# Batch 0 of a mixing-and-maxout kernel: other load order, other split of its reversed copies, more table matmuls, and a second PSUM bank for the last half block

## The chip, the cores and the metric

The kernel runs on one core of one Trainium2 chip. The core has a matrix engine (TensorE, PE in the profile), a vector engine (VectorE, DVE), a scalar engine (ScalarE, ACT), GpSimd (POOL) and SyncE (SP), which here only starts transfers. Transfers are started on three queues: SP's and ACT's (hardware queues, q1 and q10 in the profile) and POOL's (the software queue, q0). The metric is the device time of one execution in microseconds (us); lower is better.

## What is computed

The input `x` has 8 batches of 3072 x 256 numbers. Each batch goes through a two-dimensional Fourier transform of which only the real part is kept. The result, 24576 rows of 256, goes through a feed-forward layer whose hidden values are the maximum of three products.

```python
X = np.fft.fft(x, axis=1)
X = np.fft.fft(X, axis=2)
attn_out = X.real.astype(np.float32)
x = attn_out.reshape(B * S, D)
h = np.maximum(np.maximum(x @ w1, x @ w2), x @ w3)
return (h @ w_out).astype(np.float32)
```

## The kernel before

**Factoring.** The transform over 3072 rows is split as 24 times 128. Stage "s" (`Mix.s`, lines 406 to 427) does the 24-point part together with the four column groups of 64, stage "k" (`Mix.k`, 429 to 447) the 128-point part with a table of sines and cosines (`tab`). The transform over the 256 columns is folded into the weights of the layer: `prep_first` (352) and `prep_second` (373) multiply the weights with a table `md_all` and its negative `nmd_all`. After that each batch is three blocks of six units (`unit_plus`, `unit_minus`, `unit_out`), and each block is followed by its output layer (`l2_block`, 489, and `l2_last`, 532, for the last block of the last batch). A written plan (`plan`, `at`) says after which unit the stages of the next batch, the turning of its input and the loads of the batch after that are issued. Each engine then works through its own list in the order of the program.

**Input of a batch.** In memory on the chip a batch lies as 96 partitions: 4 column groups of 24 rows each. A partition holds 128 rows `bb` of 64 numbers `dl`. Stage "s" uses a column `d` twice: as it is (line 415, from `x`) and as the mirrored column of the rows in reverse order (line 417, from `back`). So a reversed copy is made: row `bb` goes to place 129 - r0 - m onward, and only `dl` 32 to 64 are needed. The reversed order also needs the row after the last one, which is the first row of the next partition: `load_next` (103) fetches these single rows in five transfers, four of 23 partitions and one of 4 partitions.

**Batch 0** is handled by code of its own, at the head of the program.

- Rows 0 to 79 come on POOL's queue, cast to bf16 on the way, straight into `x0_first` (lines 178, 186, 190), four transfers per group of rows, one per column group; then come the weights (195, 200).
- Rows 80 to 127 come as float32 on the hardware queues into three staging tiles `xs` (160 to 170): rows 80 to 95 on SP, 96 to 111 on ACT, then on SP the five one-row transfers of `load_next` and after them rows 112 to 127.
- VectorE makes the angles of `tab` (236), ScalarE the sines (249); then the small tables follow, and the angles `vm` of `md_all` (309 to 326).
- Lines 330 to 339 finish the input. For each staging tile VectorE casts it into `x0_first` (331) and ScalarE makes the reversed copy (332, recorded at line 130 in `reverse`). Then ScalarE makes the sines `md_all` (333), and five more pieces are reversed out of `x0_first`: ScalarE takes (rows 80 on, `dl` 64), (rows 0 to 30) and the lower `dl` of rows 63 to 79; VectorE takes rows 31 to 62 and the upper `dl` of rows 63 to 79.
- Before its first real work TensorE runs 17 matmuls on the table whose result is not used (line 610). The first real pair is the matmul of line 415 for column 2 and the one of line 417 behind it; 33 such pairs make stage "s" of batch 0, in seven groups; the first group needs `dl` 58 to 62 of the reversed copy, the second 53 to 57, and so on down.

**The order around the change.** A hardware transfer is given one of eight completion semaphores in turn, counted over SP and ACT together. A ninth transfer is issued when the first has landed. POOL's transfers have eight of their own.

**The end.** `l2_last` writes the last 512 rows and their mirror rows in four parts (sub 3, 0, 1, 2). Each part has two halves `h` in one PSUM tile `po` of 512 columns: six matmuls each (line 485), after two short ones (548, 550). For the last part (sub 2) each half is copied out on its own (line 554) and stored on its own (564).

Of the kernel before, what the change touches and what calls it, by code (L numbers as in the profile page):

```python
# [9 lines left out]
FP32 = mybir.dt.float32  # L10
BF16 = mybir.dt.bfloat16
# [22 lines left out]
def kernel(  # L34
# [9 lines left out]
    nc = tc.nc  # L44
# [16 lines left out]
    ps_f = ctx.enter_context(tc.tile_pool(name="ps_f", bufs=2, space=bass.MemoryType.PSUM))  # L61
    xs_pool = ctx.enter_context(tc.tile_pool(name="xs", bufs=4))
# [30 lines left out]
    def x_rows(b):  # L93
        return x[b].rearrange("(a bb) (g dl) -> g a bb dl", bb=128, g=4)

    def load_rows(eng, dst, b, r0, r1, after=None):
        xr = x_rows(b)
        for g in range(4):
            ld = eng.dma_start(out=dst[g * 24:(g + 1) * 24], in_=xr[g, :, r0:r1, :])  # L99
            if after is not None:  # L100
                tc.add_manual_dep(ld.ins, after.ins.name, AFTER, reason="weights first")

    def load_next(eng, dst, b, after=None):

        xr = x_rows(b)
        parts = [(dst[g * 24: g * 24 + 23], xr[g, 1:24, 0:1, :]) for g in range(4)]
        parts.append((dst[23:96:24], xr[:, 0, 0:1, :]))
        for (to, src) in parts:
            ld = eng.dma_start(out=to, in_=src)
            if after is not None:  # L110
                tc.add_manual_dep(ld.ins, after.ins.name, AFTER, reason="weights first")

    def load_chunk(b, ch, after=None):
        xs = xs_pool.tile([96, 33 * 64], FP32, name="xs", tag="xs")
        xv = xs.rearrange("p (bb dl) -> p bb dl", dl=64)
        load_rows(nc.sync, xv[:, 0:32 if ch == 3 else 33, :], b, ch * 32,
                  ch * 32 + (32 if ch == 3 else 33), after)
        if ch == 3:
            load_next(nc.sync, xv[:, 32:33, :], b, after)
        return xs  # L120
# [4 lines left out]
    def reverse(copy, xr, xs, r0, n, d0=32, d1=65):  # L125

        last = r0 + n > 128
        for (lo, hi, m) in ((d0, min(d1, 64), n), (64, d1, n - 1)) if last else ((d0, d1, n),):
            if lo < hi:
                copy(out=xr[:, lo - 32:hi - 32, 129 - r0 - m:129 - r0],  # L130
                     in_=bass.AP(xs.tensor, xs.offset + (m - 1) * 64 + lo,
                                 [xs.ap[0], [1, hi - lo], [-64, m]]))
# [19 lines left out]
    gen = gen_pool_cm.__enter__()  # L152
# [6 lines left out]

    x0_first = x0_pool.tile([96, 64 * 130], BF16, name="x0", tag="x0")  # L160
    x0v = x0_first.rearrange("p (bb dl) -> p bb dl", dl=64)
    staged = []
    for (r0, eng) in ((80, nc.sync), (96, nc.scalar), (112, nc.sync)):
        n = 17 if r0 == 112 else 16
        xs = xs_pool.tile([96, 33 * 64], FP32, name="xs", tag="xs")
        xv = xs[:, 0:n * 64].rearrange("p (bb dl) -> p bb dl", dl=64)
        if n > 16:
            load_next(eng, xv[:, 16:17, :], 0)
        load_rows(eng, xv[:, 0:16, :], 0, r0, r0 + 16)
        staged.append((r0, n, xs))  # L170

    pidx = gen.tile([128, 1], FP32, tag="pidx")
    iota(pidx, [[0, 1]], cm=1)
# [19 lines left out]
    for jh in range(2):  # L193
        for wsrc, wdst in ((moe_w1, w1_bf), (moe_w2, w2_bf), (moe_w3, w3_bf)):
            wld = nc.gpsimd.dma_start(
                out=wdst.rearrange("p (fc j) -> p fc j", fc=2)[:, :, jh * 384:(jh + 1) * 384],
                in_=wsrc.rearrange("(fc p) j -> p fc j", fc=2)[:, :, jh * 384:(jh + 1) * 384])
        if jh == 0:
            first_half = wld
    nc.gpsimd.dma_start(out=wout_bf.rearrange("p (jc c) -> p jc c", jc=NJC),  # L200
                        in_=moe_w_out.rearrange("(jc p) c -> p jc c", jc=NJC))
# [19 lines left out]
    half = gen.tile([128, 256], FP32, tag="half")  # L221
# [35 lines left out]
    def tab_minus(r0, r1):  # L257
        nc.vector.tensor_scalar(out=tabs[:, r0:r1, 2, :], in0=tabs[:, r0:r1, 0, :],
                                scalar1=-1.0, scalar2=None, op0=ALU.mult)
# [36 lines left out]
    for (m, c, by) in ((m24f, 0, ind24), (m24r, 24, ind24[:, ::-1])):  # L296
        nc.vector.tensor_tensor(
            out=m.rearrange("p (g r) -> p g r", g=4),
# [7 lines left out]

    tab_minus(0, 7)

    vm = gen.tile([128, 512], FP32, tag="vm")
    qm = gen.tile([128, 512], FP32, tag="qm")  # L310
    pf = gen.tile([128, 2], FP32, tag="pf")
    half = gen.tile([128, 256], FP32, tag="half")
    nc.vector.memset(half[:, 0:128], 64.0)
    nc.vector.memset(half[:, 128:256], 0.0)
    for fc in range(2):
        nc.vector.tensor_scalar(out=pf[:, fc:fc + 1], in0=pidx, scalar1=float(128 * fc),
                                scalar2=None, op0=ALU.add)
# [1 line left out]
            out=vm[:, fc * 256:(fc + 1) * 256].rearrange("p (k c) -> p k c", c=128),  # L319
# [5 lines left out]
    nc.vector.scalar_tensor_tensor(out=vm, in0=qm, scalar=-256.0 * ROUND, in1=vm,  # L325
                                   op0=ALU.add, op1=ALU.subtract)

    back = gen.tile([96, 33 * 130], BF16, tag="back")
    xr0 = back.rearrange("p (dl bb) -> p dl bb", bb=130)
    for (r0, n, xs) in staged:  # L330
        nc.vector.tensor_copy(out=x0_first[:, r0 * 64:(r0 + n) * 64], in_=xs[:, 0:n * 64])
        reverse(nc.scalar.copy, xr0, xs, r0, n, 32, 64)
    nc.scalar.activation(out=md_all, in_=vm, func=AX.Sin, scale=float(-2.0 * math.pi / 256.0))
    for (copy, r0, n, d0, d1) in ((nc.scalar.copy, 80, 49, 64, 65),
                                  (nc.scalar.copy, 0, 31, 32, 65),
                                  (nc.vector.tensor_copy, 31, 32, 32, 65),
                                  (nc.scalar.copy, 63, 17, 32, 49),
                                  (nc.vector.tensor_copy, 63, 17, 49, 65)):
        reverse(copy, xr0, x0_first[:, r0 * 64:(r0 + n) * 64], r0, n, d0, d1)
    nc.vector.tensor_scalar(out=nmd_all, in0=md_all, scalar1=-1.0, scalar2=None, op0=ALU.mult)  # L340
    tab_minus(7, 13)
    nc.vector.tensor_scalar(out=sgn, in0=pidx, scalar1=0.0, scalar2=None, op0=ALU.is_equal)
# [135 lines left out]
    def stored(st, mine, others):  # L478
        for group in others:
            tc.declare_no_dep(st.ins, group=group, reason="each store has rows of its own")  # L480
        tc.add_to_no_dep_group(mine, st.ins)

    def l2_hidden(po, hcols):
        for jc in range(NJC):
            nc.tensor.matmul(po, hcols(jc), wout_bf[:, jc * 256:(jc + 1) * 256],  # L485
                             start=False, stop=(jc == NJC - 1), skip_group_check=True)
            yield
# [44 lines left out]
    def l2_last(hp, hm, te, to, flipped):  # L532

        base = (B - 1) * S
        ter, tor = flipped
        for sub in (3, 0, 1, 2):
            slot = 8 + sub
            r = slot + 1
            cp = slice(slot * 128, slot * 128 + 128)
            sp = slice(sub * 128, sub * 128 + 128)  # L540
            sm = slice((3 - sub) * 128, (4 - sub) * 128)
            po = ps_o.tile([128, 512], FP32, name="po", tag="po")
            ot = out_pool.tile([128, 512], FP32, name="ot", tag="ot")
            for (h, tev, tov, wo, hid) in (
                    (0, te[:, cp], to[:, cp], gw[:, 256:512], lambda jc: hp[:, jc, sp]),
                    (1, ter[:, sm], tor[:, sm], gw[:, 512:768], lambda jc: hm[:, jc, sm])):
                ph = po[:, h * 256:(h + 1) * 256]
                nc.tensor.matmul(ph, tev, gw[:, 0:256], start=True, stop=False)
                yield
                nc.tensor.matmul(ph, tov, wo, start=False, stop=True)  # L550
                yield
                yield from l2_hidden(ph, hid)
                if sub == 2:
                    nc.vector.tensor_copy(out=ot[:, h * 256:(h + 1) * 256], in_=ph)
            if sub != 2:
                nc.vector.tensor_copy(out=ot, in_=po)
            if r <= 11:
                stores = [(0, 128, base + r, 0), (0, 128, base + 24 - r, 256)]
            else:
                stores = [(0, 64, base, 0), (64, 128, base + 12, 0),  # L560
                          (0, 64, base + 1548, 256), (64, 127, base + 1560, 256)]
            for k, (p0, p1, row, c) in enumerate(stores):
                eng = nc.scalar if sub == 2 and k == 0 else nc.sync
                stored(eng.dma_start(out=out[row: row + 24 * (p1 - p0 - 1) + 1: 24, :],
                                     in_=ot[p0:p1, c:c + 256]), "direct", ("scattered",))
# [40 lines left out]
                l2_queue.pop(0)  # L606

    warm = ps_s.tile([128, 512], FP32, name="warm", tag="ps")
    for _ in range(17):
        nc.tensor.matmul(warm, tab[:, 0:128], tab[:, 0:512], start=True, stop=True)  # L610
    m = Mix(0)
    x0f = (lambda d: x0v[:, 0:128, d], rows_back(xr0))
# [150 lines left out]
```

## Time and profile before

| | us |
|---|---|
| runs of the kernel before | 428.53, 429.80, 429.81 |
| median of them | 429.8 |
| the profiled execution | 428.75 |
| its span, first to last instruction | 427.0 |
| TensorE busy in it | 407.5 (95%) |
| VectorE, ScalarE, GpSimd busy | 274.1, 258.1, 244.3 |
| first real matmul of batch 0 | starts at 19.65 |
| its partner, from the reversed copy | starts at 20.65 |

The profile is of one execution. Its views name an instruction by engine, line and tiles: "L130 ACT back<-x" is the reversed copy of line 130, done by ScalarE. A number in brackets behind a row is the idle time of that engine before it and what ended it. Times in a timeline count from the start of the span, and so does every time of day in this text. The execution's own time is 1.75 us longer than the span, for what lies around it.

### The profile page before, as it was taken

Reading aid. Unit: us, or ns where it says so; the run is one execution under the profiler, and the core shown is the slowest. Engines: PE = TensorE matmul, PEld = TensorE weight load, DVE = VectorE, ACT = ScalarE, POOL = GpSimd, SP = SyncE. Lnnn points to the kernel's source line nnn. Section 1 sums busy time; section 2 is a strip of 40 time slices with the busy share of each in tenths; the row PEclk is TensorE's granted clock in tenths of the full one; section 3 lists DMA queues with packets and bytes.
Section 4 is the critical chain, followed back from the end, with each engine's and each line's share of the span. In section 5 each row is a group of like instructions: output and inputs, shape, how many; then the busy total and the mean of one; then the engine's idle time right before and its main releaser. Section 6 shows DMA issues by size and latency. Waiting matters only on the chain.

```text
span 427.0 us, 8732 instructions
## 1 busy us (share of the span) xinstructions
PE 407.5 (95%) x3073; PEld 271.5 (64%) x3073; DVE 274.1 (64%) x455; ACT 258.1 (60%) x477; POOL 244.3 (57%) x291
## 2 busy tenths in 40 slices
PE   0699999999999999999999999999999999999996
PEld 0275667666676666666666666666666666666665
DVE  8747566565666665676656665675656665666773
ACT  6736666666666666656665566647665666655550
POOL 9639655973279625983289624983289622214320
PEclk9989999999999999999999999999999999999999
DMA  9998893594217941498217851387311221212223
GB/s 131 130 170 176 169 230 111 141 217 103 98 72 169 202 134 52 109 206 168 99 61 169 207 141 51 96 199 179 107 55 71 64 74 63 74 51 58 93 74 124
DMA packets 130180, 52.28 MB, mean 122 GB/s; under 512 B 112081, under 2 KB 127192, under 8 KB 130136
## 3 DMA queue, kind: packets, MB, share of 16 engines
q1 hardware_dynamic: 107784, 36.52, 36.6%
q0 software_dynamic: 20624, 14.68, 15.0%
q10 hardware_dynamic: 1728, 0.52, 0.6%
q8 instruction: 24, 0.39, 0.4%
q14 instruction: 20, 0.16, 0.1%
HBM read 29.02 MB, written 25.17 MB: 127 GB/s over the span
## 4 chain that ended last, share of the span: by engine, by line
PE 94%; POOL 2%; DMA 2%; ACT 1%; DVE 0%; issue 0%; POOLq 0%
PE po L485 29%; PE pse L461 15%; PE pse L462 15%; PE pse L469 14%; PE po L509 5%; PE ps L415 3%; PE ps L417 3%; PE ps L443 3%; PE ps L441 2%; PE pl L501 2%; POOL x L99 2%; DMA x<-in_x_dram 2%; PE psg L361 1%; ACT back L130 0%; PE pst L380 0%
## 5 line engine op out<-in xcount | busy, mean ns | idle before, releaser
L475 ACT ACTIVATE stmp<-pse 128x512 bf16<-128x512 f32 x288 | 171.5, 600 | 52.7 <-PE pse L462 47.0
L519 POOL DMA_INDIRECT out_dram<-ot,rows_m x92 | 100.4, 1091 | 160.7 <-DVE ot L514 145.0
L476 DVE TENSOR_TENSOR hp<-pse,stmp 128x512 bf16<-128x512 f32 x144 | 99.5, 691 | 129.8 <-ACT stmp L475 91.4
L461 PE MATMUL pse<-t,gE 128*128 128x512 bf16 x288 | 109.2, 379 | 1.0 <-ACT gO L368 0.6
L462 PE MATMUL pse<-t,gO 128*128 128x512 bf16 x288 | 109.0, 378 | 0.0
L476 DVE TENSOR_TENSOR hm<-pse,stmp 128x512 bf16<-128x512 f32 x144 | 99.2, 689 | 6.8 <-ACT stmp L475 6.7
L485 PE MATMUL po<-wout_bf,hp 128*128 128x256 bf16 x576 | 86.1, 273 | 0.0
L469 PE MATMUL pse<-t,gD 128*128 128x512 bf16 x288 | 85.6, 379 | 0.0
L485 PE MATMUL po<-wout_bf,hm 128*128 128x256 bf16 x576 | 78.6, 273 | 0.0
L485 PEld LDWEIGHTS <-hp 128*128 128x128 bf16 x576 | 56.4, 98 | 26.1
L485 PEld LDWEIGHTS <-hm 128*128 128x128 bf16 x576 | 56.4, 98 | 16.3
L514 DVE TENSOR_TENSOR ot<-po,even 128x512 f32<-128x512 f32 x92 | 62.8, 683 | 0.0
L145 POOL CAST x<-xs 96x1056 bf16<-96x1056 f32 (+1 forms) x35 | 58.3, 1677 | 0.0
L143 POOL CAST x<-xs 96x1056 bf16<-96x1056 f32 x28 | 56.7, 2027 | 0.0
L445 ACT CAST t<-ps 128x512 bf16<-128x512 f32 x47 | 27.5, 586 | 43.3 <-PE ps L443 43.1
L422 ACT CAST z_all<-ps 128x480 bf16<-128x480 f32 x45 | 25.2, 559 | 43.1 <-PE ps L417 43.1
L469 PEld LDWEIGHTS <-gD 128*128 128x128 bf16 x288 | 27.9, 98 | 32.2
L462 PEld LDWEIGHTS <-gO 128*128 128x128 bf16 x288 | 28.1, 98 | 20.4 <-issue 2.0
L461 PEld LDWEIGHTS <-gE 128*128 128x128 bf16 x288 | 28.1, 98 | 19.5 <-issue 0.4
L509 PE MATMUL po<-gw,t 128*128 128x512 bf16 x92 | 34.9, 379 | 0.0
L415 PE MATMUL ps<-m24f,x 96*128 96x96 bf16 (+1 forms) x256 | 29.8, 213 | 2.0 <-DMA w_bf<-in_moe_w_dram 2.0
L415 PEld LDWEIGHTS <-x 96*128 96x128 bf16 x264 | 25.3, 106 | 3.0 <-DVE back L130 2.5
(137 smaller groups left out, 325.4 us busy)
## 6 DMA issues: line engine op xcount, KB each, us to landing
xs<-in_x_dram SPq DMA_DIRECT2D x84, 198.0 KB
out_dram<-ot SPq DMA_DIRECT2D x90, 128.0 KB
xs<-in_x_dram SPq DMA_DIRECT2D x28, 192.0 KB
out_dram<-ot,rows_m POOLq DMA_INDIRECT x92, 2.9
w_bf<-in_moe_w_dram POOLq DMA_DIRECT2D x6, 192.0 KB, 5.7
out_dram<-ot SPq DMA_DIRECT2D x17, 64.0 KB
xs<-in_x_dram SPq DMA_DIRECT2D x8, 96.0 KB
x<-in_x_dram POOLq DMA_DIRECT2D x8, 96.0 KB, 7.9
```

What stands on the lines that cost most here:

```text
L143: nc.gpsimd.tensor_copy(v[:, 0:33, ch * 32:ch * 32 + 32], xs[:, 0:32 * 64].rearrange("p (bb dl) -> p dl bb", dl=64)[:, 0:33, :])
L145: reverse(lambda out, in_: nc.gpsimd.tensor_copy(out, in_), v[:, 33:66, :], xs, ch * 32, 33 if ch == 3 else 32)
L415: nc.tensor.matmul(ps1[:, c0:c0 + n], x0[0](d), mf[:, 0:n], start=True, stop=False)
L461: nc.tensor.matmul(pse[:, 0:n], gE[i][:, js], te, start=True, stop=False)
L462: nc.tensor.matmul(pse[:, 0:n], gO[i][:, js], to, start=False, stop=True)
L469: nc.tensor.matmul(pse, gD[i][:, js], to, start=False, stop=True, skip_group_check=True)
L475: nc.scalar.activation(out=stmp[:, 0:n], in_=pses[0][:, 0:n], func=AX.Relu)
L476: nc.vector.tensor_tensor(out=dst, in0=src3, in1=stmp[:, 0:n], op=ALU.max)
L485: nc.tensor.matmul(po, hcols(jc), wout_bf[:, jc * 256:(jc + 1) * 256], start=False, stop=(jc == NJC - 1), skip_group_check=True)
L509: nc.tensor.matmul(po, to[:, cp], gw[:, 256:768], start=True, stop=True)
L514: nc.vector.tensor_tensor(out=ot.rearrange("p (h c) -> p h c", h=2), in0=po.rearrange("p (h c) -> p h c", h=2), in1=lin.unsqueeze(1).to_br ...
L519: stored(nc.gpsimd.indirect_dma_start(out, bass.IndirectOffsetOnAxis(ap=rows_m[0:128 - lo, b * 12 + slot: b * 12 + slot + 1], axis=0), ot[ ...
```

## The change

Four things are changed at the head and one at the end.

1. Loads of rows 80 to 127. Rows 112 to 127 go to ACT's queue, as its only loads. On SP the four one-row transfers of 23 partitions come first, then rows 80 to 111 as four transfers of 32 rows into one staging tile, then the one-row transfer of 4 partitions. There are two staging tiles now: `xs_a` with 17 rows (112 to 127 and the one-row transfers) and `xs_b` with 32 rows.
2. The casts of the staging tiles into `x0_first` move from VectorE to ScalarE, and their reversed copies from ScalarE to VectorE.
3. VectorE does these reversed copies ahead of the angles `vm`, not behind them. The five later pieces are split in another way: ScalarE takes rows 0 to 30 ahead of the sines `md_all`, and `dl` 54 to 64 of rows 31 to 79 behind them; VectorE takes the rest. A second tile of constants (two memsets) falls away.
4. 27 table matmuls in place of 17.
5. In `l2_last` the second half of the last part gets a PSUM tile of its own, out of another pool.

```diff
--- before.py
+++ after.py
@@ -100,12 +100,14 @@
             if after is not None:
                 tc.add_manual_dep(ld.ins, after.ins.name, AFTER, reason="weights first")
 
-    def load_next(eng, dst, b, after=None):
+    def load_next(eng, dst, b, after=None, mid=None):
 
         xr = x_rows(b)
         parts = [(dst[g * 24: g * 24 + 23], xr[g, 1:24, 0:1, :]) for g in range(4)]
         parts.append((dst[23:96:24], xr[:, 0, 0:1, :]))
-        for (to, src) in parts:
+        for k, (to, src) in enumerate(parts):
+            if k == 4 and mid is not None:
+                mid()
             ld = eng.dma_start(out=to, in_=src)
             if after is not None:
                 tc.add_manual_dep(ld.ins, after.ins.name, AFTER, reason="weights first")
@@ -159,15 +161,12 @@
 
     x0_first = x0_pool.tile([96, 64 * 130], BF16, name="x0", tag="x0")
     x0v = x0_first.rearrange("p (bb dl) -> p bb dl", dl=64)
-    staged = []
-    for (r0, eng) in ((80, nc.sync), (96, nc.scalar), (112, nc.sync)):
-        n = 17 if r0 == 112 else 16
-        xs = xs_pool.tile([96, 33 * 64], FP32, name="xs", tag="xs")
-        xv = xs[:, 0:n * 64].rearrange("p (bb dl) -> p bb dl", dl=64)
-        if n > 16:
-            load_next(eng, xv[:, 16:17, :], 0)
-        load_rows(eng, xv[:, 0:16, :], 0, r0, r0 + 16)
-        staged.append((r0, n, xs))
+    xs_a, xs_b = [xs_pool.tile([96, 33 * 64], FP32, name="xs", tag="xs") for _ in range(2)]
+    rows = lambda t, r0, r1: t[:, r0 * 64:r1 * 64].rearrange("p (bb dl) -> p bb dl", dl=64)
+    load_rows(nc.scalar, rows(xs_a, 0, 16), 0, 112, 128)
+    load_next(nc.sync, rows(xs_a, 16, 17), 0, mid=lambda: load_rows(
+        nc.sync, rows(xs_b, 0, 32), 0, 80, 112))
+    staged = [(112, 17, xs_a), (80, 32, xs_b)]
 
     pidx = gen.tile([128, 1], FP32, tag="pidx")
     iota(pidx, [[0, 1]], cm=1)
@@ -306,12 +305,19 @@
 
     tab_minus(0, 7)
 
+    back = gen.tile([96, 33 * 130], BF16, tag="back")
+    xr0 = back.rearrange("p (dl bb) -> p dl bb", bb=130)
+
+    def turn_rows(copy, r0, n, d0, d1):
+        reverse(copy, xr0, x0_first[:, r0 * 64:(r0 + n) * 64], r0, n, d0, d1)
+
+    for (r0, n, xs) in staged:
+        nc.scalar.copy(out=x0_first[:, r0 * 64:(r0 + n) * 64], in_=xs[:, 0:n * 64])
+        reverse(nc.vector.tensor_copy, xr0, xs, r0, n, 32, 64)
+
     vm = gen.tile([128, 512], FP32, tag="vm")
     qm = gen.tile([128, 512], FP32, tag="qm")
     pf = gen.tile([128, 2], FP32, tag="pf")
-    half = gen.tile([128, 256], FP32, tag="half")
-    nc.vector.memset(half[:, 0:128], 64.0)
-    nc.vector.memset(half[:, 128:256], 0.0)
     for fc in range(2):
         nc.vector.tensor_scalar(out=pf[:, fc:fc + 1], in0=pidx, scalar1=float(128 * fc),
                                 scalar2=None, op0=ALU.add)
@@ -325,18 +331,12 @@
     nc.vector.scalar_tensor_tensor(out=vm, in0=qm, scalar=-256.0 * ROUND, in1=vm,
                                    op0=ALU.add, op1=ALU.subtract)
 
-    back = gen.tile([96, 33 * 130], BF16, tag="back")
-    xr0 = back.rearrange("p (dl bb) -> p dl bb", bb=130)
-    for (r0, n, xs) in staged:
-        nc.vector.tensor_copy(out=x0_first[:, r0 * 64:(r0 + n) * 64], in_=xs[:, 0:n * 64])
-        reverse(nc.scalar.copy, xr0, xs, r0, n, 32, 64)
+    turn_rows(nc.scalar.copy, 0, 31, 32, 65)
+    turn_rows(nc.vector.tensor_copy, 80, 49, 64, 65)
     nc.scalar.activation(out=md_all, in_=vm, func=AX.Sin, scale=float(-2.0 * math.pi / 256.0))
-    for (copy, r0, n, d0, d1) in ((nc.scalar.copy, 80, 49, 64, 65),
-                                  (nc.scalar.copy, 0, 31, 32, 65),
-                                  (nc.vector.tensor_copy, 31, 32, 32, 65),
-                                  (nc.scalar.copy, 63, 17, 32, 49),
-                                  (nc.vector.tensor_copy, 63, 17, 49, 65)):
-        reverse(copy, xr0, x0_first[:, r0 * 64:(r0 + n) * 64], r0, n, d0, d1)
+    for (r0, n) in ((31, 32), (63, 17)):
+        turn_rows(nc.scalar.copy, r0, n, 54, 65)
+        turn_rows(nc.vector.tensor_copy, r0, n, 32, 54)
     nc.vector.tensor_scalar(out=nmd_all, in0=md_all, scalar1=-1.0, scalar2=None, op0=ALU.mult)
     tab_minus(7, 13)
     nc.vector.tensor_scalar(out=sgn, in0=pidx, scalar1=0.0, scalar2=None, op0=ALU.is_equal)
@@ -544,6 +544,8 @@
             for (h, tev, tov, wo, hid) in (
                     (0, te[:, cp], to[:, cp], gw[:, 256:512], lambda jc: hp[:, jc, sp]),
                     (1, ter[:, sm], tor[:, sm], gw[:, 512:768], lambda jc: hm[:, jc, sm])):
+                if sub == 2 and h == 1:
+                    po = ps_f.tile([128, 512], FP32, name="pol", tag="ps")
                 ph = po[:, h * 256:(h + 1) * 256]
                 nc.tensor.matmul(ph, tev, gw[:, 0:256], start=True, stop=False)
                 yield
@@ -606,7 +608,7 @@
                 l2_queue.pop(0)
 
     warm = ps_s.tile([128, 512], FP32, name="warm", tag="ps")
-    for _ in range(17):
+    for _ in range(27):
         nc.tensor.matmul(warm, tab[:, 0:128], tab[:, 0:512], start=True, stop=True)
     m = Mix(0)
     x0f = (lambda d: x0v[:, 0:128, d], rows_back(xr0))
```

## The prediction, made before the changed kernel was run

> **What bounds the kernel now.** I read the page first. TensorE is busy 95% of the span, and the slices of the second part put its idle time at the head:
>
> ```profile
> PE   0699999999999999999999999999999999999996
> PEclk9989999999999999999999999999999999999999
> ```
>
> The first slice has no matmul, the last is short, and the clock dips in the third. TensorE's waits after 29 us sum to 1.3 us, 0.5 of it at the end. So in between nothing absorbs or adds time: what the head gives or takes reaches the end whole, and so does the tail.
>
> Next I read the chain of waits up to 32 us. It follows POOL's loads of x, then a DMA landing, then ScalarE's reversed copies, then the first pair:
>
> ```profile
> 12.04 6.55 DMA x<-in_x_dram
> 18.58 2.02 ACT back L130 x2
> 20.60 0.05 issue
> 20.65 0.22 PE ps L417
> ```
>
> ScalarE's timeline shows what stands ahead of that copy:
>
> ```profile
> 16.88 1.18 ACT L130 CAST back<-xs 96x544 bf16<-96x544 f32 x1 [2.82 <-DMA xs<-in_x_dram]
> 17.96 0.63 ACT L333 ACTIVATE md_all<-vm 128x512 bf16<-128x512 f32 x1
> ```
>
> ScalarE sits idle 2.82 us until the last staging tile has landed at 16.88. From then it works without a gap to 20.59, and TensorE starts at 20.65: **3.77 us from landing to start.** Rows 0 to 30 were in long before; they only stand behind in ScalarE's list.
>
> Why does it land that late? SyncE's list of issues, then packets, MB and share of the queues in the stretches 8:10 (one line) and 11:16 (us):
>
> ```profile
> 0.74 1.81 SPq L99 DMA_DIRECT2D xs<-in_x_dram  x4
> 3.76 3.04 SPq L109 DMA_DIRECT2D xs<-in_x_dram  x5
> ```
>
> ```profile
> q1 hardware_dynamic: 61, 0.02, 4.9%
> ```
>
> ```profile
> q0 software_dynamic: 3293, 0.32, 106.4%
> q1 hardware_dynamic: 1413, 0.35, 47.3%
> ```
>
> After four transfers each on SP and ACT, the ninth waits for the first landing (3.76). Then q1 carries almost only one-row packets in 8:10, while rows 112 on are queued behind them. In 11:16 it moves 283 packets per us beside POOL's queue.
>
> **The loads.** The new order gives the eight completion slots to ACT's four transfers (rows 112 to 127) and four one-row transfers. SP's first 32-row transfer is the ninth and waits for ACT's first. In before the first landed 3.0 us after its issue at 0.74, so I expect about 3.7 again, and its packets from about 5.0 (1.25 us after issue: the first packets of before show just before 2.0). These four transfers are 4 x 24 x 32 = 3072 packets of 256 B. The fifth one-row transfer (1 KB) is behind them in the same queue, and **both the cast and the reversed copy of `xs_a` read its row**. So `xs_a`, first in both engines' lists, can be taken up only when `xs_b` lands too. Call that time L.
>
> Bounds for L. Slow end: 283 packets per us throughout, 10.9 us, plus 0.8 from the last packets to the casts (about 16.05, as 16:17 holds only 14 more, to 16.88): 16.7. [...] Alone, q1 moved 846 in 28:29 (14 ns per packet on each of the 12 engines that a 24-partition load lands on by the trace's DMA events); alone, q0 moved 1409 in 8:9 (11 ns on 16). [...] I take 15.3: POOL's queue has only half the hardware loads ahead of it and so gets a start, which leaves q1 about 390 per us (midway from 283 to the 496 of 5:6) for 3 us, and 283 after that. This is nearer to the slow end, whose row has the same queues on the same engines.
>
> [...]
>
> **From L to the first pair.** ScalarE's list in after: cast 1088 numbers, cast 2048, reversed copy of rows 0 to 30, sines, two pieces of 352 and 187. Casts by L253's rows (896 in 0.95, 768 in 0.84, so 0.9 ns per number): 1.12 and 1.99. Rows 0 to 30 cost 1.94 and the sines 0.63, as now. The pieces lie between rows of 48 (0.26), 289 (0.68) and 512 (1.08): 0.79 and 0.50. That is 6.97, less five overlaps of about 0.09: 6.5, plus 0.06 to TensorE. **The start is L + 6.6**, against 3.77 behind the landing now: more of ScalarE's work stands behind it. For L = 15.3 it is 21.9, later by 1.25 us.
>
> VectorE's copies of the staging tiles have no row. The nearest are bf16 copies of its own (1056 in 1.13, 272 in 0.40), so 0.65 and 1.10; ScalarE's 512 float32 in 1.06 gives 1.13 and 2.1. I take the first, being the same engine. Then the `vm` group (11.77 to 14.60 now, 2.83) ends at L + 4.6. ScalarE comes to the sines at L + 4.8, so this added wait is covered by 0.2 us; at the dear end it costs 1.3 us, with two pieces behind it and TensorE behind those. VectorE's own later pieces serve column 11 on (after nine pairs, 1.2 us) and end at about L + 6.1: hidden. POOL's issues keep their order; the removed memsets (0.34 us) leave idle time.
>
> **The clock.** Windows of the trace; the third number from the end is the granted clock:
>
> ```profile
> 20.00:23.00 3.00, 2.35 (x35) 2.36 (x36) 1.26 (x5) 1.96 (x4) 2.69 (x8) 0.96 1.08 150
> 22.70:26.10 3.40, 3.40 (x40) 3.05 (x40) 1.38 (x3) 1.50 (x4) 0.43 (x2) 0.51 1.22 159
> ```
>
> TensorE ran its table matmuls to 17.6, then one matmul in 3 us, and from 22.7 to 26.1 was granted half clock. A pair took 0.160 us in place of 0.134: 16.5 pairs lose 0.43, and four weight products after them 0.40 (1.05 against 0.65). Cost now: 0.83. Ten more table matmuls at 0.216 end at 19.77; they are free while the start is later (L over 13.1). For a start at 21.9 the gap is 2.1 us, and I expect half clock over the same stretch, now on 21 pairs: 0.55, a gain of 0.28. If it stays full, the gain is 0.83.
>
> [...]
>
> **The tail.**
>
> ```profile
> 422.01 0.44 DVE ot L554
> 422.44 0.04 issue
> 422.49 0.27 PE po L548
> ```
>
> The second half's first matmul waits for the copy of the first half, though it writes other columns of the tile. Its weights were in at 421.80, so it loses 0.69. With a tile of its own it goes on at once, the last copy ends at 423.29, and SP, whose earlier issues end at 423.06, is free. Bound: 0 to 0.69; I take 0.69, as nothing else is late there.
>
> **Sum.** Head +1.25, clock -0.28, tail -0.69: +0.28 us, on the profiled execution's 428.75: 429.0. The median shown stands 1.05 above that execution, the mean of all four at 429.2; from the middle I forecast **429.3**, no change.
>
> **The rivals.**
>
> - **Early landing.** [...] Chance 0.34.
> - **Slower, by the one-row transfer.** `xs_a` is held by the last 1 KB behind 786 KB, ScalarE idles from 12.1 to L, and all 6.6 us stand behind it. It decides from L = 16.4. At 16.7 the start is 23.3, +2.65 - 0.38 - 0.69 = +1.6: 430.3; a late `vm` adds up to 1.3. For it: the measured rate and the fixed order. Against it: the lighter traffic before 8 us. Chance 0.27.
> - **Only the clock holds**, L as forecast: +1.25 - 0.83 - 0.69 = -0.27, 428.5. [...] Chance 0.05.
> - My forecast, L from 14.1 to 16.3: 0.34. The start then lies between 20.7 and 22.9, and with half clock lasting as said the profiled time between 427.8 and 430.0.
>
> A difference of 0.3% (1.3 us) is about what a measurement of this kernel can tell from none. Faster by more: 0.34. Within: 0.34 + 0.05 = 0.39. Slower by more: 0.27. The range takes in most of both sides, moved by the spread of the runs: 426.9 to 431.3; the likeliest case alone gives 428.1 to 430.3 on the same scale as 429.3.
>
> **What would show it.** L is the start of ScalarE's first cast of `xs` at the head; if it is under 14, the rate is wrong. TensorE's first L417 at L + 6.6 proves ScalarE's sum; sines that wait for `vm` show VectorE dearer. PEclk in the third slice shows the clock. No idle time before the last L548 shows the tail. The forecast fails if the fifth one-row transfer does not land with `xs_b`, or if POOL's last x rows move.

## The result, and the profile after

| | before | after |
|---|---|---|
| median of 22 runs each | 429.63 us | 431.19 us |
| lowest to highest | 428.53 to 430.24 | 427.84 to 432.08 |
| ratio, 95% interval | | 1.003 [1.0018, 1.0043] |
| profiled execution, its span | 428.75, 427.0 | 430.91, 429.1 |

The change makes the kernel slower by 0.3%. The forecast of no difference was wrong: the interval of the ratio leaves out 1, and the kernel moved the way of the second rival. The time lies in the forecast's range (426.9 to 431.3), 0.1 us from its end; that range took in most of the rivals too, so this says nothing for the mechanism.

TensorE's busy share is the same, 95%. The third slice of its clock has changed:

```profile
PE   0789999999999999999999999999999999999997
PEclk9969999999999999999999999999999999999999
```

ScalarE's timeline at the head, to compare with the rows of line 130 in the forecast:

```profile
16.17 2.90 ACT L315 CAST x<-xs 96x1088 bf16<-96x1088 f32 x2 [4.06 <-DMA xs<-in_x_dram]
18.98 1.98 ACT L132 COPY back<-x 96x1023 bf16<-96x1023 bf16 x1
20.85 0.64 ACT L336 ACTIVATE md_all<-vm 128x512 bf16<-128x512 f32 x1
21.39 1.21 ACT L132 COPY back<-x 96x352 bf16<-96x352 bf16 x2
```

ScalarE waits 4.06 us, until 16.17, and then has 6.4 us of work in one piece. TensorE is done with its table at about 20.0 and waits for the last of it:

```profile
11.71 8.29 PE L612 MATMUL warm<-tab 128*128 128x512 bf16 x27 [11.71 <-DVE tab L257]
19.84 0.21 PE L415 MATMUL ps<-m24f,x 96*128 96x96 bf16 x1
22.65 0.22 PE L417 MATMUL ps<-m24r,back 96*128 96x96 bf16 x1 [2.60 <-ACT back L132]
```

The first pair is complete at 22.65, against 20.65: 2.00 us later. SyncE's queue, where L111 are the one-row transfers and L99 the 32-row ones:

```profile
0.74 1.38 SPq L111 DMA_DIRECT2D xs<-in_x_dram  x4
2.16 6.34 SPq L99 DMA_DIRECT2D xs<-in_x_dram  x4
8.55 2.26 SPq L111 DMA_DIRECT2D xs<-in_x_dram  x1
```

The fifth one-row transfer is issued only at 8.55. In the trace's DMA events its four engines report between 15.48 and 15.92, behind the last 32-row transfer (15.26). Rows 112 to 127 themselves had all reported by 7.73 and the four other one-row transfers by 5.19. So the first tile in both lists stands complete but for 1 KB for 8.2 us.

The clock, in windows of after (the third number from the end is the granted clock):

```profile
20.00:22.60 2.60, 0.05 (x2) 0.00 (x0) 2.56 (x8) 2.59 (x4) 2.36 (x6) 1.00 1.16 160
23.30:26.60 3.30, 3.30 (x45) 3.30 (x44) 1.31 (x2) 1.12 (x2) 0.00 (x0) 0.50 1.32 184
26.70:30.00 3.30, 3.30 (x24) 2.09 (x22) 1.21 (x2) 0.91 (x3) 0.00 (x0) 0.50 0.89 169
```

and of before:

```profile
22.80:26.10 3.30, 3.30 (x39) 2.95 (x38) 1.32 (x2) 1.48 (x4) 0.33 (x2) 0.50 1.23 160
26.20:30.00 3.80, 3.23 (x23) 2.22 (x22) 1.77 (x3) 1.50 (x3) 1.25 (x1) 1.00 1.10 193
```

In this execution of after half clock lasts 6.83 us (23.23 to 30.05), in that of before 3.41 (22.76 to 26.17). From the first pair to the first unit (line 461) it is 10.37 us in after (22.65 to 33.02) and 9.31 in before (20.65 to 29.96); an execution with full clock needs 8.53 (19.24 to 27.77, experiment e9 below). So half clock costs 1.84 and 0.78 us in these two.

The end, from the chain of after:

```profile
425.03 0.11 PE pol L550
425.14 0.11 PE pol L552
425.25 0.67 PE pol L485 x6
425.92 0.02 issue
425.94 0.42 DVE ot L556
```

The last half follows without a wait. From the first copy to the second it is 0.87 us (425.07 to 425.94), against 1.55 (422.01 to 423.56): 0.68 saved.

The two profiled executions thus differ by +2.00 (start) + 1.06 (clock) - 0.68 (tail) = +2.38 us, of which the spans show 2.1; the rest is after the last copy, where what follows it takes 0.3 us less.

### The profile page after: what moved, and what is told of

Same layout as the page of the kernel before. It is cut to its first block, busy times and chain, and to the rows that moved or that the text cites. A ratio compares the mean times of both kernels' runs of the same rounds, so it can differ in the third digit from the quotient of the medians.

```text
span 429.1 us, 8683 instructions
## 1 busy us (share of the span) xinstructions
PE 407.6 (95%) x3028; PEld 273.0 (64%) x3083; DVE 273.0 (64%) x453; ACT 258.2 (60%) x476; POOL 244.8 (57%) x291
## 4 chain that ended last, share of the span: by engine, by line
PE 84%; DMA 5%; DVE 3%; issue 2%; ACT 2%; POOL 1%; SPq 1%; DVEq 0%; ACTq 0%; POOLq 0%
PE po L485 27%; PE pse L461 14%; PE pse L469 13%; PE pse L462 12%; PE po L509 4%; PE ps L443 2%; PE ps L441 2%; PE ps L415 2%; PE ps L417 2%; DMA x<-in_x_dram 2%; PE pl L501 2%; DMA xs<-in_x_dram 2%; PE psg L361 1%; DVE ot L514 1%; ACT stmp L475 1%
## 5 line engine op out<-in xcount | busy, mean ns | idle before, releaser
L461 PE MATMUL pse<-t,gE 128*128 128x512 bf16 x285 | 108.0, 379 | 2.8 <-ACT gO L368 0.6
L462 PE MATMUL pse<-t,gO 128*128 128x512 bf16 x255 | 96.5, 379 | 0.2
L469 PE MATMUL pse<-t,gD 128*128 128x512 bf16 x274 | 82.6, 379 | 0.4
L485 PE MATMUL po<-wout_bf,hm 128*128 128x256 bf16 x570 | 77.7, 273 | 0.3
L485 PEld LDWEIGHTS <-hm 128*128 128x128 bf16 x576 | 56.4, 98 | 16.3
L509 PE MATMUL po<-gw,t 128*128 128x512 bf16 x87 | 33.0, 379 | 0.0
L505 ACT COPY even<-pl 128x512 f32<-128x512 f32 x46 | 26.8, 582 | 0.1
```

The costliest lines, as they stand in the source:

```text
L461: nc.tensor.matmul(pse[:, 0:n], gE[i][:, js], te, start=True, stop=False)
L462: nc.tensor.matmul(pse[:, 0:n], gO[i][:, js], to, start=False, stop=True)
L469: nc.tensor.matmul(pse, gD[i][:, js], to, start=False, stop=True, skip_group_check=True)
L509: nc.tensor.matmul(po, to[:, cp], gw[:, 256:768], start=True, stop=True)
```

## The experiments

Each was timed in five rounds beside the kernel before on one chip; ratios are to that kernel, with 95% intervals. "Start" is the first matmul of line 417 of batch 0 (or its new line number) in the profile.

| run | median | before on that chip | ratio | start |
|---|---|---|---|---|
| a, the change again | 430.71 | 429.63 | 1.0031 [1.0017, 1.0045] | 22.25 |
| e1, fifth one-row first | 429.41 | 430.32 | 0.9984 [0.9969, 0.9999] | 21.50 |
| e2, tail alone | 429.76 | 430.32 | 0.9989 [0.9975, 1.0003] | 20.99 |
| e3, 39 table matmuls | 429.93 | 430.32 | 0.9992 [0.9978, 1.0006] | 23.25 |
| e4, loads alone | 430.44 | 428.71 | 1.0035 [1.0015, 1.0055] | 21.31 |
| e5, copies alone | 431.18 | 428.71 | 1.0049 [1.0031, 1.0067] | 22.40 |
| e6, reordered | 427.55 | 430.32 | 0.9944 [0.9924, 0.9964] | 20.03 |
| e7, before with 31 tables | 428.35 | 429.63 | 0.9971 [0.9960, 0.9982] | 21.19 |
| e8, reordered, fifth second | 426.64 | 428.71 | 0.9940 [0.9922, 0.9958] | 20.00 |
| e9, e8 with 17 tables | 425.91 | 428.71 | 0.9928 [0.9910, 0.9945] | 19.24 |
| e10, e7 and tail | 428.68 | 429.99 | 0.9964 [0.9950, 0.9977] | 20.62 |
| e11, e9 without tail | 428.33 | 429.99 | 0.9951 [0.9933, 0.9969] | 19.75 |

**The change again.**

> The changed kernel once more beside the kernel before on one chip, to have its time beside those of the experiments. Theory: 1.3 us longer than before, ratio 1.002 to 1.0045, and in the profile half clock for one or two stretches of 3.4 us from about 23 us on. Rival (the difference belongs to one chip or hour): ratio within 0.001 of 1.

The ratio is the same. The runs also list each execution's granted clock (mean over the span), and that sorts the spread. Of 21 runs of before in this set, 16 have 0.992 or less (mean 429.8) and 5 have 0.994 or more (428.6); of 12 of after, 9 have 0.992 or less (431.0) and 3 have 0.995 or more (430.0). At like clock (executions of one group compared with each other) after is 1.3 to 1.4 us slower, which is about the start's delay less the tail. In this set half clock costs both kernels about alike, and the profiled execution of before (0.994) was of its luckier group. The shares of the groups change from set to set, though: before has 0.992 or less in 4 of 14 executions beside e4 and in 17 of 29 beside e1, so the ratios of the table carry some clock.

**e1: is it the fifth one-row transfer?** An edit of the changed kernel:

```diff
-    load_next(nc.sync, rows(xs_a, 16, 17), 0, mid=lambda: load_rows(
-        nc.sync, rows(xs_b, 0, 32), 0, 80, 112))
+    load_next(nc.sync, rows(xs_a, 16, 17), 0)
+    load_rows(nc.sync, rows(xs_b, 0, 32), 0, 80, 112)
```

> The changed kernel with the fifth one-row transfer issued right behind the other four, ahead of the 32-row transfers. Theory (the staging tile with rows 112 to 127 is held until 16.2 us by one transfer of 1 KB): its cast starts when ScalarE is free at about 12.0 us, the other tile is cast when it lands at 15.3 to 15.7, and the first pair starts about 5.5 us behind that, near 21.0 in place of 22.65; the time falls by 1.6 us or more, to about 429.0 to 429.6. Rival (the landing does not matter, ScalarE's longer list does): the cast still ends the list as late, and the time stays within 0.5 us of the changed kernel's 431.2.

```profile
12.72 1.08 ACT L315 CAST x<-xs 96x1088 bf16<-96x1088 f32 x1
15.73 1.90 ACT L315 CAST x<-xs 96x2048 bf16<-96x2048 f32 x1 [1.93 <-DMA xs<-in_x_dram]
17.54 1.98 ACT L132 COPY back<-x 96x1023 bf16<-96x1023 bf16 x1
19.70 0.64 ACT L336 ACTIVATE md_all<-vm 128x512 bf16<-128x512 f32 x1 [0.18 <-DVE vm L331]
```

The first cast no longer waits; the second starts when its tile is in. The start is 21.50, 1.15 us earlier, and the ratio goes from 1.003 to 0.9984: some 2 us, with intervals apart. Not all of it is the landing, since five of the twelve runs of e1 had full clock and only one of the 34 of the changed kernel did. At like clock e1 is level with before (430.6 each at 0.992 or less, 429.3 and 429.4 at 0.994 to 0.996), so the transfer's place is worth some 1.2 to 1.5 us. The theory holds against its rival. Two things came out dearer than expected, and the start is 0.5 us behind the expected 21.0. With five one-row transfers first, the ninth hardware transfer is one of ACT's own, and ScalarE's list waits for a slot: its table load starts at 4.41 in place of 3.07, and all that follows there is 0.7 late. And the sines waited 0.18 us for `vm`.

**e2: the tail alone.** Before, with the last hunk of the change only.

> The kernel before with the second PSUM tile for the last half and nothing else. Theory: the 0.69 us wait ahead of the last six matmuls goes, the end comes 0.69 us earlier: 428.9 against 429.6, ratio 0.9984. Rival (the end is set by the first half's store, or the new tile waits for another): no change.

The wait is gone from TensorE's list of waits, and the ratio is 0.9989 with an interval that holds both 0.9984 and 1. By itself this does not decide. At like clock e2 is 0.3 us faster (0.992 or less, 7 runs against 17 of before) and 0.5 us (0.994 or more, 5 against 12).

**e10 and e11: the tail in two other kernels.** e10 is before with 31 table matmuls and the tail's hunk; e11 is the reordered kernel of e9 without that hunk.

> The kernel before with 31 table matmuls and the second PSUM tile for the last half. With 31 table matmuls alone its granted clock was near full in all runs, so the tail's share is not buried in the spread that the clock makes (ratio 0.9971 against before). Theory: 0.69 us less than that, ratio 0.9955. Rival (the tail's wait hides behind the last stores): 0.9971 again.

> The reordered kernel with 17 table matmuls (ratio 0.9928 against before, full clock in five of six runs), with one PSUM tile for the last part as before the change. Theory: 0.69 us more, ratio 0.9944, and a wait of 0.5 us ahead of the last half in the profile. Rival (the tail is hidden): 0.9928 again.

e10 is 0.0007 under e7 (0.3 us, from two chips), e11 0.0023 over e9 (1.0 us). The intervals of these differences hold the expected 0.0016, and neither leaves out zero. They are not clean pairs either: in the profiled executions e10 starts 0.57 us earlier than e7, and e11 starts 0.51 us later than e9 and waits 1.4 us for POOL's `gD` where e9 waits 0.6, and its clock was 0.996 in three of six runs. TensorE's waits show the wait where the hunk is missing and not where it is there; e11:

```profile
PE pse L476 <- POOL gD L376: 1.4, 1, 1.4
PE po L555 <- DVE ot L561: 0.5, 1, 0.5
```

So the 0.68 us is read off the traces, and the three timed pairs agree in sign; none of them measures its size.

**e3 and e7: the clock.** e3 is the changed kernel with 39 table matmuls, e7 the kernel before with 31. The "thin pairs" of the texts are the pairs of stage "s" with their 96 columns:

```diff
-    for _ in range(17):
+    for _ in range(31):
```

> The changed kernel with 39 table matmuls in place of 27, so that they end at about 22.5 us and TensorE goes into the first pairs without a gap. Theory (the profiled execution of the changed kernel loses 1.9 us to half clock between 23.2 and 30.1, against 0.8 before): the clock stays full, the start of the pairs stays near 22.7, and the time falls by about 1.9 us to 429.3. Rival (the clock falls through the thin pairs themselves, whatever runs before them): half clock in the record as now, and 431.2 again. Second rival (more table matmuls hold up the start): the start moves behind 22.7 and the time rises.

> The kernel before with 31 table matmuls in place of 17 and nothing else; they end at about 20.6 us, when the first pair starts. Theory: no gap, the clock stays full in the profile, the start stays at 20.7 and the time falls by 0.8 us or more (ratio 0.998 or less). Rival (the clock falls through the thin pairs whatever runs ahead of them): half clock as before, ratio 1.

In e7 the clock is 0.998 or more in nine of nine runs, and the ratio is 0.9971, although the tables now end after ScalarE and hold the start up to 21.19. Its clock:

```profile
21.20:25.50 4.30, 4.30 (x67) 4.30 (x66) 1.48 (x3) 1.74 (x4) 1.68 (x6) 1.00 1.08 146
25.60:30.00 4.40, 3.83 (x28) 2.54 (x26) 2.16 (x4) 1.89 (x5) 1.48 (x2) 1.00 1.13 185
```

In e3 the clock is full in ten of twelve runs; the profiled one is of the other two. There L (the start of the first cast) was 16.74 and the start 23.25, not 22.7, so a gap of 1 us was left behind the tables, and half clock came once (0.50 in the window from 25.9 to 29.2). The time falls by 0.4% from the change's 1.003, some 1.6 us where 1.9 was expected. So the thin pairs alone do not bring the clock down; idle time of TensorE ahead of them has a part in it (0.99 us in the profile of e3, 2.60 in that of after; the clock was full in ten of the twelve executions of e3 and in one of the 34 of after). How much it takes is not shown: e9 below kept full clock in five of six runs with 1.6 us between its tables and its first matmul.

**e4 and e5: loads or copies?** e4 has the new loads with the old copies (and without the two memsets), e5 the old loads with the new copies; both have 17 table matmuls and the old tail.

> The kernel before with the new order of loads alone (two staging tiles, fifth one-row transfer last); casts on VectorE, reversed copies on ScalarE, 17 table matmuls and the tail as before. Theory: the tile with the one-row transfers is up at about 16.2 us, ScalarE then has 0.5 + 1.0 k numbers of reversed copies, sines and rows 0 to 30 ahead of the start, 5.4 us, so the first pair starts near 21.7, 1.0 us later than before; with the clock's share the time is 1.0 to 2.0 us longer (ratio 1.0025 to 1.0045). Rival (the new order lands earlier and the loss is in the new split of the copies): the start is at 20.6 or earlier and the ratio at or below 1.

> The kernel before with the new split and order of the copies alone (casts on ScalarE, reversed staging copies and then the angles vm on VectorE); loads, 17 table matmuls and the tail as before. Theory: the third staging tile lands at about 17.0, VectorE reverses it and only then makes vm until 20.4, ScalarE's sines and two pieces wait for that, so the start is near 22.2, 1.5 us later: ratio 1.0035 or more. Rival (the split is the good part and the loads the bad one): two tiles are cast and reversed ahead of 16 us, the start is before 20.6, ratio below 1.

Both are slower than before by themselves. ScalarE in e4, then in e5:

```profile
15.61 3.11 ACT L132 CAST back<-xs 96x544 bf16<-96x544 f32 x2 [3.51 <-DMA xs<-in_x_dram]
18.63 0.62 ACT L329 ACTIVATE md_all<-vm 128x512 bf16<-128x512 f32 x1
19.16 2.67 ACT L132 COPY back<-x 96x48 bf16<-96x48 bf16 x3
```

```profile
17.14 1.10 ACT L318 CAST x<-xs 96x1088 bf16<-96x1088 f32 x1 [3.16 <-DMA xs<-in_x_dram]
18.15 1.98 ACT L132 COPY back<-x 96x1023 bf16<-96x1023 bf16 x1
20.62 0.63 ACT L339 ACTIVATE md_all<-vm 128x512 bf16<-128x512 f32 x1 [0.48 <-DVE vm L334]
21.15 1.20 ACT L132 COPY back<-x 96x352 bf16<-96x352 bf16 x2
```

In e4 the landing is 1.3 us earlier than before (15.61 against 16.88), and it buys nothing: two tiles, not one, are then reversed behind it, and 5.7 us pass to the start at 21.31. In e5 ScalarE needs 5.3 us from the landing, 0.48 of it for `vm`, which VectorE now makes last. The clock has a part in both ratios: all runs of e4 and e5 have 0.992 or less, and of the 14 runs of before beside them only four. Against those four (mean 430.05) e4 is 0.3 us slower and e5 1.1. So e4's loss is small at like clock: its ratio met the expected 1.0025 to 1.0045 with the clock's share, while its start came at 21.31 where 21.7 was expected. Neither half of the change was the good one.

**e6, e8, e9: the same pieces in the order of their landing.** e6 takes the five one-row transfers first, `vm` ahead of VectorE's copies, and this order on ScalarE, with 26 table matmuls:

```diff
+    cast(*staged[0])
+    turn_rows(nc.scalar.copy, 0, 31, 32, 65)
+    nc.scalar.activation(out=md_all, in_=vm, func=AX.Sin, scale=float(-2.0 * math.pi / 256.0))
+    cast(*staged[1])
...
```

e8 has the fifth one-row transfer behind the first 32-row one, and 27 table matmuls; e9 is e8 with 17.

> The changed kernel with the fifth one-row transfer first, the angles vm ahead of the reversed copies on VectorE, ScalarE's order cast of rows 112 on, rows 0 to 30, sines, cast of rows 80 to 111, the two late pieces, and 26 table matmuls. Theory: nothing but a cast of 2.0 us and two pieces of 1.2 us stands behind the landing of rows 80 to 111 at 15.3 to 15.7, POOL's last rows of x (18.6) plus 0.5 set the start at about 19.3 to 19.9, the clock holds, and the time is about 426.5 (ratio 0.993). Rival (ScalarE's sum sets the start, whatever its order): a start behind 21 us and 429 or more.

> The reordered kernel (vm first on VectorE, rows 0 to 30 and the sines ahead of the big cast on ScalarE) with 27 table matmuls and the fifth one-row transfer behind the first 32-row transfer, not ahead of all four. Theory (with five one-row and four ACT transfers first, the ninth issue is one of ACT's, and ScalarE's sines of the table begin 0.7 us later): the first table matmul is back at 11.7 from 12.6, the start is at about 19.6 to 20.0, and the clock holds: 427 or less, as the other reordered kernel or up to 0.5 us better. Rival (the fifth transfer again lands late, behind 32-row packets): a cast of rows 112 on that starts behind 13 us.

> The same with 17 table matmuls, which end near 17.6 us. Theory (table matmuls up to the start keep the clock full): the start is the same, half clock appears in the record for one or two stretches of 3.4 us, and the time is 0.8 to 1.9 us longer than with 27. Rival (the early start alone keeps the clock): full clock, the same time.

All three are faster than both kernels. e6 and e1 were timed on one chip and differ in the order, in `vm` and in one table matmul: together these take the start from 21.50 to 20.03 and the ratio from 0.9984 to 0.9944. e6 came out 1 us above its expected 426.5; its table was as late as in e1, and its last piece waited for POOL's rows until 19.43. In e8 the tables begin at 11.89 (12.61 in e6), as expected, but its big tile landed at 16.84 in that execution, and the start stayed at 20.00, where the tables end. e9 has the lowest ratio, 0.9928, though its interval and those of e6 and e8 overlap, and its expectation fell: half clock did not come (full in five of six runs). Its ScalarE, less one piece of 0.78 us at 17.41:

```profile
12.01 1.08 ACT L335 CAST x<-xs 96x1088 bf16<-96x1088 f32 x1
13.00 1.98 ACT L132 COPY back<-x 96x1023 bf16<-96x1023 bf16 x1
14.88 0.62 ACT L339 ACTIVATE md_all<-vm 128x512 bf16<-128x512 f32 x1
15.60 1.90 ACT L335 CAST x<-xs 96x2048 bf16<-96x2048 f32 x1
18.66 0.53 ACT L132 COPY back<-x 96x187 bf16<-96x187 bf16 x1 [0.47 <-DMA x<-in_x_dram]
```

It works from 12.0 with hardly a wait, the last piece waits for POOL's last rows of x, and the start is 19.24. With POOL's landing as the bound, 27 table matmuls would end 0.7 us after this start (from the 8.23 us that they took in e8).

## Why the prediction was wrong

1. **What bounds the kernel.** Right. What the head and the tail gave or took came out at the end.
2. **L = 15.3: the step that failed.** It was 16.17, 15.76 in the repeat and 16.74 in e3, near the slow end, 16.7, or just past it. The mean, 16.2, is 0.9 us behind the forecast, and that is most of the 1.3 us between the forecast's +0.28 and the medians' +1.56. The working's own rates and its 0.8 us at the end give 15.5, not 15.3. Those rates were 390 packets per us for 3 us from 5.0, then 283. The queue began earlier: it moved 636 packets in 3:5, then 186, 46 and 422 in the three microseconds from 5. By 8.0 some 1230 packets of the 32-row transfers were through, where the working had 1170. The time was lost after that, with 1895 in 8:16, 237 per us:

```profile
q0 software_dynamic: 6425, 0.61, 142.1%
q1 hardware_dynamic: 1895, 0.48, 40.2%
```

   The queue nearly stood still twice, in 6:7 and, what cost the time, from 11.0 to 12.5, with 108 packets (the row is 11:12):

```profile
q1 hardware_dynamic: 46, 0.01, 7.1%
```

```profile
q1 hardware_dynamic: 63, 0.01, 8.2%
```

   The first time SyncE was at the issue of the fourth large transfer (4.93 to 8.50); the second time its last issue had ended at 10.81, so the issue did not hold it up. Why the queue stood still was not tried and stays open. The forecast also had the first large transfer wait for one of ACT's: its issue began at once (2.16), when none of ACT's had landed (the first at 3.25). So the traffic began earlier than forecast and still ended later.
3. **The start at L + 6.6.** Right: 6.48, 6.49 and 6.51 in three executions. VectorE's copies took 1.65 us together (1.75 forecast), and the sines were ready in time in after, with the small margin forecast; in e1 and e5 they were not.
4. **The clock, a gain of 0.28.** Wrong too. In the profiled pair it was a loss of 1.06, as half clock stayed for 6.83 us in place of 3.41. Over all runs there was no gain: 0.992 or less, where 0.992 is the mean of the execution with 6.83 us at half clock, is listed for 26 of the 34 executions of after and for 45 of the 79 of before. The step took one execution's half clock for the kernel's. In after half clock came behind a gap of 2.60 us; in the profile of e9 it did not come behind one of 1.59.
5. **The tail, 0.69.** Right (0.68).
6. **The sum.** With the measured start (+1.9, the mean of 22.65, 22.25 and 23.25 against that of 20.65 and 20.99), the tail (-0.68) and no difference of clock it is +1.2; the medians moved by 1.56, the like-clock means by 1.3 to 1.4. The forecast had 0.28. The rest of the 1.56 may be clock: five of the 22 executions of after behind its median had 0.988 (some 10 us at half clock by an estimate, as 3.41 us of it take 0.004 off the mean over 429 us), and none of before was under 0.990.
7. **The rivals.** The second rival was the right one in its mechanism, as e1 shows. In its place in L it was not: it was put to decide from L = 16.4, while 16.17 and 15.76 lie in the interval of the forecast's own case (14.1 to 16.3), and the time moved by 0.3% all the same. That interval counted on a gain of clock that did not come. The early landing, L of 14.0 or less, did not come either: no execution with the fifth one-row transfer last shows it (16.17, 15.76, 16.74 and, in e4, 15.61).

## What to carry to other kernels

Count an engine's work from the last landing it needs, not its total: e4 landed 1.3 us earlier and started 0.66 later (21.31 against 20.65), since it put more behind the landing, and the reordered kernels won by doing the pieces that had landed first (starts from 19.24 to 20.03). A tile is as late as its last transfer, however small: in after 1 KB held one up for 8.2 us. So this load belongs ahead of the big ones of its queue, but look which engine's issue then waits for a completion slot (in e1 it was ScalarE's, whose table load began at 4.41 in place of 3.07). Before a stage at the head is priced by its clock, look at several executions (those of before beside e1 had 0.990 to 0.996), and compare kernels at like clock.

## What was not expected of the hardware

How long half clock lasted. In after the granted clock rises at 16.40, falls to half at 23.23 and is back at 30.05; in before the times are 15.93, 22.76 and 26.17. So full clock lasted 6.83 us in both, and half clock twice as long in after (6.83) as in before (3.41). In after it held through 96-column pairs up to 27.6 and then through 2.4 us of 384-column products. In before it was lifted 0.8 us after these products had begun (25.36). Two more profiles lie between, by the times of their matmuls: in e4 half clock was lifted some 0.6 us after these products had begun (26.41 to 27.0), in e2 it held from 22.7 to some 29.5, with the products from 25.81 on. What ends half clock is not shown by this. The same kernel ran from 427.84 us (clock 1.000) to 432.08 (0.988); that the time at which half clock sets in does this alone is not shown, as L moved too (15.76 to 16.74).
